# First batch of a retention scan: the state's decay moved to VectorE, half of the key scaling moved to ScalarE

## The chip, the cores and the metric

The kernel runs on one core of a Trainium2 chip. Five engines work side by side, each with its own queue that it takes in order: TensorE (PE in the profile) multiplies matrices into PSUM, VectorE (DVE), ScalarE (ACT) and GpSimd (POOL) work on tiles of 128 partitions, and SyncE (SP) issues the DMAs. They wait for each other by semaphores. The metric is the device time of one launch in microseconds (us), the median of 3 runs.

## The reference

Three blocks follow one another. The first is a causal linear attention with decay over 2 batches, 8 heads, 768 positions and head size 64. The two others are a Fourier mixing block with an MLP and a normalised MLP on the 512 features that result.

```
for b in range(nb):                      # blocks along the sequence
    intra = (qb @ kb.T) * Dmask          # within the block, decay by distance
    intra = intra @ vb
    inter = (qb * lam_pow) @ kv_state    # what earlier blocks left
    out[block] = intra + inter
    kb_dec = kb * rev_pow                # keys, scaled by position in the block
    kv_state = lam_block * kv_state + kb_dec.T @ vb
x = u + mlp(norm(u)), u = out + real(fft2(out))
x = x + mlp(norm(x) * g)
```

## The kernel before, in words

The attention handles chunks of 128 positions, six in each batch; the first batch runs first and alone, in about the first 33 us. For each chunk c of it:

- `attn_a` (lines 338 to 357) scales the keys, kd = k * rev0, by one GpSimd multiply over all 8 heads (line 344), and converts v into a high and a low half (vhl) on ScalarE and VectorE (lines 348, 349).
- `attn_scores` and `attn_x` (lines 363 to 383): TensorE forms the scores of even and odd heads in two PSUM banks. VectorE multiplies each bank with the decay mask (line 377), ScalarE rounds the result to 16 bits (the cast of line 380), GpSimd subtracts to get the low half (line 382). The low half of chunk c and head parity e is `m{c}_{e}` below.
- `attn_s_steps` (from line 470) advances the state, one 64x64 matrix for each head, kept as 128x256 (four pairs of heads). TensorE forms kd.T @ v in PSUM (line 486). In the first batch ScalarE decays the old state beforehand by four 128x64 multiplies, one for each pair (line 477), and VectorE adds the two (line 496). ScalarE then copies the state onto the block diagonals of `diag` (line 501).
- `attn_i_steps` multiplies the next chunk's queries with `diag` (line 399), VectorE scales that into `int` (line 403).
- `attn_o_steps` multiplies m with vhl (line 450), and VectorE writes the sum of that and `int` to u (lines 454, 456).

In the second batch GpSimd does both the key scaling and the decay (line 479); it is not touched.

Up to the output of chunk 3 a scheduler in the framework sets the order on each engine when the program is built; for what is left of the first batch the table ORDER sets it by hand (its token `s` is one step of `attn_s_steps` for chunk 4, O4, O5 and I are steps of the outputs and of the last product), until the first MLP block starts. Behind the change, the order of the instructions on every engine is the same before and after from about the end of the first batch on, and so is the order of all DMAs on SyncE.

Of the kernel before, what the change touches and what calls it, by code (L numbers as in the profile page):

```python
# [14 lines left out]
AF = mybir.ActivationFunctionType  # L15
ALU = mybir.AluOpType
# [3 lines left out]
P = 128  # L20
B, H, S, D = 2, 8, 768, 64
# [105 lines left out]
def tile_retention_fourier_mlp(ctx: ExitStack, tc: tile.TileContext, a: dict, out: bass.AP):  # L127
    nc = tc.nc
    pe, act, dve, pool, sp = nc.tensor, nc.scalar, nc.vector, nc.gpsimd, nc.sync
# [18 lines left out]
    def bank(which, name):  # L148
        return banks[which].tile([P, 512], F32, tag=which, name=name)

    def f32t(name, spare=None):
        if spare is not None:
            return wpool.tile([P, 512], F32, tag=f"w2_{spare}", name=name)
        return fp.tile([P, 512], F32, tag="f", name=name)

    def hl(name):
        return fp.tile([P, 2, 512], F16, tag="f", name=name)
# [17 lines left out]
    loaded = {}  # L175

    def load(b, c, names=("kt", "qt", "v", "k")):
        for nm in names:
            n = ("kt", "qt", "v", "k").index(nm)
            if b == 0 and c >= 2:  # L180
                t = wpool.tile([P, 512], F32, tag=f"w2_{(4 * (c - 1) + n) % 16}", name=f"{nm}{b}_{c}")
            else:
                t = ldp.tile([P, 512], F32, tag="ld", name=f"{nm}{b}_{c}")
            sp.dma_start(t, a[nm][b, c])
            loaded[nm, b, c] = t
# [14 lines left out]
    lc = const.tile([P, H // 2], F32, name="lc")  # L200
# [5 lines left out]
    rev = const.tile([P, H], F32, name="rev")  # L206
    dve.tensor_scalar(rev, last, QS, None, op0=ALU.mult)
    rev0 = const.tile([P, H], F32, name="rev0")
# [129 lines left out]
    def attn_a(b, c, bk):  # L338
        if b > 0 and c + 2 < NCH:
            load(b, c + 2)  # L340
        kd = None
        if c < NCH - 1:
            kd = f32t(f"kd{b}_{c}")
            pool.tensor_tensor(kd.rearrange("p (h d) -> p h d", h=H), loaded["k", b, c].rearrange("p (h d) -> p h d", h=H),  # L344
                               (rev if b else rev0).unsqueeze(2).to_broadcast([P, H, D]), op=ALU.mult)
        v_ = loaded["v", b, c]
        t = hl(f"vhl{b}_{c}")
        act.activation(t[:, 0], v_, AF.Copy, scale=QS)
        dve.scalar_tensor_tensor(t[:, 1], v_, QS, t[:, 0], op0=ALU.mult, op1=ALU.subtract)
        vs[b, c] = t  # L350
        if kd is not None and b == 0:
            ks[b, c] = kd
        elif kd is not None:
            t = hl(f"khl{b}_{c}")
            act.copy(t[:, 0], kd)
            pool.tensor_tensor(t[:, 1], kd, t[:, 0], op=ALU.subtract)
            ks[b, c] = t
# [111 lines left out]

    def attn_s_steps(b, c, bk):  # L470
        new, old = states[c % 2], states[(c - 1) % 2]
        if c > 0:
            dec = stp.tile([P, H // 2 * D], F32, tag="dec", name=f"dec{b}_{c}")
            do, di = (z.rearrange("p (i d) -> p i d", d=D) for z in (dec, old))
            if b == 0:
                for i in range(H // 2):
                    act.activation(do[:, i], di[:, i], AF.Copy, scale=lc[:, i:i + 1])
            else:
                pool.tensor_tensor(do, di, lc.unsqueeze(2).to_broadcast([P, H // 2, D]), op=ALU.mult)
        yield  # L480
        k_ = ks[b, c]
        ps = bank(bk["st"], f"ps_st{b}_{c}")
        for h in range(H):
            (i, e), hc = divmod(h, 2), slice(h * D, (h + 1) * D)
            if b == 0:
                pe.matmul(ps[e * D:(e + 1) * D, i * D:(i + 1) * D], k_[:, hc], loaded["v", b, c][:, hc], start=True, stop=True)
                continue
            for n, (x, y) in enumerate(PASS):
                pe.matmul(ps[e * D:(e + 1) * D, i * D:(i + 1) * D], k_[:, x, hc], vs[b, c][:, y, hc],
                          start=n == 0, stop=n == 2)  # L490
        yield
        psv = ps[:, :H // 2 * D]
        if c == 0:
            dve.tensor_copy(new, psv)
        else:
            dve.tensor_tensor(new, psv, dec, op=ALU.add)
        yield
        if b == 0:
            for e in range(2):
                r = slice(e * D, (e + 1) * D)  # L500
                act.copy(diag[c % 2][r, :, e * D:(e + 1) * D], new[r].rearrange("p (i d) -> p i d", d=D))
        yield

    def attn_c(b, c, bk):
        run(attn_o_steps(b, c, bk))
        if c < NCH - 1:
            run(attn_s_steps(b, c, bk))
# [729 lines left out]
    def attn_seq(b, bk):  # L1237
        seq = {"ab": [(attn_a, 0), (attn_a, 1), (attn_b, 0)], "ba": [(attn_b, 0), (attn_a, 0), (attn_a, 1)],
               "aba": [(attn_a, 0), (attn_b, 0), (attn_a, 1)]}[AO]
        for c in range(NCH):  # L1240
            seq.append((attn_c, c))
            if c + 2 < NCH:
                seq.append((attn_a, c + 2))
            if c + 1 < NCH:
                seq.append((attn_b, c + 1))
                seq.append((attn_i, c + 1))
        return [lambda f=f, c=c: f(b, c, bk) for f, c in seq]
# [41 lines left out]
    def eng(n):  # L1289
        return pool if n in ONPOOL.split() else dve  # L1290

    wide = {}
    chains = {"s": lambda: attn_s_steps(0, 4, bk0), "O4": lambda: attn_o_steps(0, 4, bk0),
              "O5": lambda: attn_o_steps(0, 5, bk0), "I": lambda: attn_i_steps(0, 5, bk0), "R": lambda: row_fold(0)}
    for x in range(2):
# [85 lines left out]
    n = t + DC + DFO  # L1381
# [107 lines left out]
```

## Time and profile before

| | |
|---|---|
| median of 3 runs | 583.66 us (583.55 to 583.71) |
| profiled execution, its own time | 584.53 us |
| its span, first to last instruction | 582.7 us |
| TensorE busy | 564.7 us, 97% |
| VectorE busy | 405.3 us, 70% |
| GpSimd busy | 341.6 us, 59% |
| ScalarE busy | 303.0 us, 52% |

The table is over the whole span. The first 33 us look otherwise: in them GpSimd is nearly as busy as TensorE, and VectorE follows closely, so a share of the whole span says little about the stage that is changed. The profiled execution took 584.53 us, 1.83 us more than its span and 0.87 us more than the median; sums from its rows are made against its own time.

### The profile page before, as it was taken

What the parts mean: (1) busy time and instruction counts of PE and PEld (TensorE: products, weight loads), DVE (VectorE), ACT (ScalarE), POOL (GpSimd) and SP (SyncE); (2) the same over time, 40 slices, a digit from 0 to 9 for tenths busy, and PEclk for the clock granted to TensorE, in tenths of its full rate; (3) what the DMA queues carried; (4) which work ended last, traced back from release to release, by engine and by line L of the source; (5) the groups of instructions that cost most, each with busy time, mean ns of one, the idle gap of its engine ahead of it and who ended that gap; (6) DMA issues with size and microseconds to landing.
All of it is one profiled execution on the core that took longest, in us unless ns stands there. A gap on an engine that the chain in (4) does not pass through costs nothing.

```text
span 582.7 us, 12211 instructions
## 1 busy us (share of the span) xinstructions
PE 564.7 (97%) x4718; PEld 385.0 (66%) x4718; DVE 405.3 (70%) x921; ACT 303.0 (52%) x624; POOL 341.6 (59%) x364
## 2 busy tenths in 40 slices
PE   7989998999999999999999999999999999999997
PEld 4745654666554555677777667666777788878884
DVE  6898898867876449678677766656756665756544
ACT  4867779743232333465597888954242453223320
POOL 7825699985553565365366877754196676223511
PEclk9998999999999999999999999999999999999999
DMA  8999079960000011243365453400120025002001
GB/s 281 369 362 368 19 253 253 334 206 23 1 0 1 10 38 27 74 127 109 83 183 171 131 183 125 141 20 1 55 56 1 19 91 56 2 1 78 34 1 55
DMA packets 47018, 63.26 MB, mean 109 GB/s; under 512 B 26225, under 2 KB 29167, under 8 KB 46959
## 3 DMA queue, kind: packets, MB, share of 16 engines
q1 hardware_dynamic: 46142, 62.27, 34.4%
q8 instruction: 37, 0.61, 0.4%
q10 hardware_dynamic: 816, 0.21, 0.2%
q14 instruction: 23, 0.18, 0.1%
HBM read 52.23 MB, written 6.29 MB: 100 GB/s over the span
## 4 chain that ended last, share of the span: by engine, by line
PE 63%; DVE 12%; POOL 12%; ACT 6%; issue 5%; DMA 1%; SPq 0%; DVEq 0%; POOLq 0%; ACTq 0%
PE ps_y L919 25%; PE ps L868 21%; PE ps_h L759 5%; POOL w L332 4%; POOL m L382 3%; PE ps_y L966 2%; DVE wr L792 1%; PE ps_d L558 1%; PE ps_b L966 1%; PE ps_a L966 1%; POOL kd L344 1%; PE ps_h L749 1%; ACT half L304 1%; DVE tr L815 1%; ACT w L330 1%
## 5 line engine op out<-in xcount | busy, mean ns | idle before, releaser
L919 PE MATMUL ps_y<-w,h 128*128 128x512 f16 (+1 forms) x1026 | 248.1, 377 | 1.7 <-ACT h L904 1.1
L919 PEld LDWEIGHTS <-h 128*128 128x128 f16 x1032 | 98.2, 98 | 88.8 <-ACT h L904 2.5
L868 PEld LDWEIGHTS <-sw 128*128 128x128 f16 x1104 | 94.6, 98 | 20.5 <-issue 2.6
L868 PE MATMUL ps<-th,sw 128*128 128x192 f16 x756 | 86.0, 246 | 1.6 <-DVE wf L307 0.7
L332 POOL TENSOR_TENSOR w<-wf,w 128x512 f16<-128x512 f32 x58 | 66.8, 1159 | 26.8 <-ACT w L330 26.6
L868 PEld LDWEIGHTS <-w 128*128 128x128 f16 x828 | 71.0, 98 | 11.2 <-issue 0.2
L759 PE MATMUL ps_h<-unT,w 128*128 128x384 f16 x396 | 72.3, 326 | 0.7 <-ACT w L330 0.7
L868 PE MATMUL ps<-unT,w 128*128 128x192 f16 x552 | 61.9, 246 | 0.0
L759 PEld LDWEIGHTS <-w 128*128 128x128 f16 x396 | 37.6, 98 | 29.4 <-ACT w L330 1.6
L804 POOL TENSOR_TENSOR sw<-ws,sw 128x512 f16<-128x512 f32 x32 | 37.0, 1174 | 21.2 <-ACT sw L803 21.2
L330 ACT CAST w<-wf 128x512 f16<-128x512 f32 x58 | 35.3, 611 | 12.3 <-DVE wf L317 9.3
L1154 ACT ACTIVATE h<-ps 128x384 f16<-128x384 f32 x44 | 21.7, 496 | 34.3 <-DVE ps L1161 29.7
L382 POOL TENSOR_TENSOR m<-m,m 128x512 f16<-128x512 f32 x24 | 31.7, 1336 | 7.1 <-ACT m L380 5.1
L307 DVE SCALAR_TENSOR_TENSOR wf<-ws,ps_w 128x512 int32<-128x512 int32 x34 | 23.2, 685 | 17.2 <-ACT ps_w L305 6.9
L701 POOL TENSOR_TENSOR rs<-rs,neghalf 128x1 f32<-128x1 f32 x24 | 14.3, 601 | 35.2 <-DVE rs L699 35.2
L833 POOL TENSOR_TENSOR th<-ts,th 128x384 f16<-128x384 f32 x22 | 20.5, 951 | 24.0 <-ACT th L832 22.8
L905 DVE SCALAR_TENSOR_TENSOR h<-ps,h 128x384 f16<-128x384 f32 x48 | 25.6, 553 | 12.7 <-ACT h L904 12.2
L1183 POOL TENSOR_TENSOR hh<-s,hh 128x256 f16<-128x256 f32 x22 | 14.3, 675 | 32.9 <-ACT hh L1182 30.9
L722 POOL TENSOR_TENSOR uns<-un,uns 128x512 f16<-128x512 f32 x21 | 25.2, 1199 | 12.9 <-ACT uns L721 12.9
L904 ACT ACTIVATE h<-ps 128x384 f16<-128x384 f32 x48 | 22.4, 486 | 19.6 <-DVE ps L898 16.0
L774 DVE SCALAR_TENSOR_TENSOR h<-ps_h,h 128x384 f16<-128x384 f32 x36 | 19.7, 549 | 18.1 <-ACT h L773 18.0
L868 PE MATMUL ps<-unT,sw 128*128 128x192 f16 x276 | 30.3, 246 | 0.0
(223 smaller groups left out, 1040.3 us busy)
## 6 DMA issues: line engine op xcount, KB each, us to landing
ws<-in_w SPq DMA_DIRECT2D x25, 511.8 KB, 5.0
ws<-in_w2b SPq DMA_DIRECT2D x16, 511.8 KB, 4.0
ws<-in_w1b SPq DMA_DIRECT2D x16, 511.8 KB, 3.9
kt<-in_kt SPq DMA_DIRECT2D x12, 256.0 KB, 6.3
qt<-in_qt SPq DMA_DIRECT2D x12, 256.0 KB, 5.5
v<-in_v SPq DMA_DIRECT2D x12, 256.0 KB, 5.3
k<-in_k SPq DMA_DIRECT2D x12, 256.0 KB, 4.8
pre<-in_w SPq DMA_DIRECT2D x4, 511.8 KB, 9.7
```

What stands on the lines that cost most here:

```text
L307: dve.scalar_tensor_tensor(ti, raw[:, :, 0], 13, part.bitcast(I32), op0=ALU.logical_shift_right, op1=ALU.bitwise_or)
L330: act.copy(hi, t)
L332: gate["lo"] = pool.tensor_tensor(lo, t, hi, op=ALU.subtract)
L382: pool.tensor_tensor(t[:, 1], m32, t[:, 0], op=ALU.subtract)
L722: pool.tensor_tensor(s_[:, 1], un, s_[:, 0], op=ALU.subtract)
L759: pe.matmul(ps, w[:, i, k, fo:fo + P], x[:, j, k, :], start=n == 0, stop=n == 11)
L804: pool.tensor_tensor(lo, z, hi, op=ALU.subtract)
L868: pe.matmul(ps, lhs, rhs, start=start and n == 0, stop=n == 5, skip_group_check=True)
L904: gate["relu"] = act.activation(hi, z, AF.Relu)
L905: dve.scalar_tensor_tensor(lo, z, 0.0, hi, op0=ALU.max, op1=ALU.subtract)
L919: pe.matmul(ps, h[:, x, j * P:(j + 1) * P], w[:, y, c], start=f == first and n == 0, stop=f == NF - 1 and n == 2, skip_group_check=True)
L966: pe.matmul(ps[:, c], lhs[:, x], rhs[:, y], start=start == 1 and n == 0 and p == 0, stop=n == 2, skip_group_check=True)
```

## The change

For the first batch the separate decay tile is gone: VectorE computes old * lc + PSUM for one pair of heads at a time, four instructions of 128x64 (lc holds one decay factor for each partition and pair). The scaled keys are computed in two parts: heads 4 to 7 by GpSimd in one multiply of 128x256, heads 0 to 3 by ScalarE in four multiplies of 128x64.

```
@@ attn_a
         kd = None
         if c < NCH - 1:
             kd = f32t(f"kd{b}_{c}")
-            pool.tensor_tensor(kd.rearrange("p (h d) -> p h d", h=H), loaded["k", b, c].rearrange("p (h d) -> p h d", h=H),
-                               (rev if b else rev0).unsqueeze(2).to_broadcast([P, H, D]), op=ALU.mult)
+            ko, ki = (z.rearrange("p (h d) -> p h d", h=H) for z in (kd, loaded["k", b, c]))
+            r_, n = (rev, 0) if b else (rev0, H // 2)
+            pool.tensor_tensor(ko[:, n:], ki[:, n:], r_[:, n:].unsqueeze(2).to_broadcast([P, H - n, D]), op=ALU.mult)
+            for h in range(n):
+                act.activation(ko[:, h], ki[:, h], AF.Copy, scale=r_[:, h:h + 1])
@@ attn_s_steps
         new, old = states[c % 2], states[(c - 1) % 2]
-        if c > 0:
+        if c > 0 and b > 0:
             dec = stp.tile([P, H // 2 * D], F32, tag="dec", name=f"dec{b}_{c}")
             do, di = (z.rearrange("p (i d) -> p i d", d=D) for z in (dec, old))
-            if b == 0:
-                for i in range(H // 2):
-                    act.activation(do[:, i], di[:, i], AF.Copy, scale=lc[:, i:i + 1])
-            else:
-                pool.tensor_tensor(do, di, lc.unsqueeze(2).to_broadcast([P, H // 2, D]), op=ALU.mult)
+            pool.tensor_tensor(do, di, lc.unsqueeze(2).to_broadcast([P, H // 2, D]), op=ALU.mult)
...
         if c == 0:
             dve.tensor_copy(new, psv)
+        elif b == 0:
+            for i in range(H // 2):
+                r = slice(i * D, (i + 1) * D)
+                dve.scalar_tensor_tensor(new[:, r], old[:, r], lc[:, i:i + 1], psv[:, r], op0=ALU.mult, op1=ALU.add)
         else:
             dve.tensor_tensor(new, psv, dec, op=ALU.add)
```

The scheduler places the new instructions and moves some of the old ones. Three places matter. The first is the start of ScalarE's queue. In the names the first number is the chunk (vhl_0 belongs to chunk 0, m_0_1 to chunk 0 and odd heads), the last one is the buffer. A wait on DMAHW5 is one for v of chunk 0, a wait on DMAHW6 one for k of chunk 0. Before:

```order
L348 ACT_TABLE_LOAD
L348 ACTIVATE vhl_0_205<-v_0_125 128x512 [waits DMAHW5_49]
L380 CAST m_0_0_225<-m_0_0_0_221 128x512 [waits DVE_49]
L380 CAST m_0_1_228<-m_0_0_1_223 128x512 [waits DVE_49]
L348 ACTIVATE vhl_1_233<-v_1_142 128x512 [waits DMAHW1_49]
L501 COPY diag<-state_161 64x4x64 [waits DVE_49]
```

The same place now:

```order
L348 ACT_TABLE_LOAD [waits DMAHW6_49]
L348 ACTIVATE kd_0_203<-k_0_127,rev_154 128x64 [waits DVE_49]
L348 ACTIVATE kd_0_203<-k_0_127,rev_154 128x64 x3
L351 ACTIVATE vhl_0_209<-v_0_125 128x512 [waits DMAHW5_49]
L383 CAST m_0_0_229<-m_0_0_0_225 128x512 [waits DVE_49]
L383 CAST m_0_1_232<-m_0_0_1_227 128x512 [waits DVE_49]
L348 ACTIVATE kd_1_235<-k_1_144,rev_154 128x64 [waits DMAHW2_49]
```

The four multiplies on k of chunk 0 stand in front of v and of the first cast, and the load of ScalarE's function table, which waited for nothing, now stands behind the wait for k. The second place is GpSimd, from the first scaled keys to the low halves of chunk 2. Before:

```order
L344 TENSOR_TENSOR kd_0_203<-k_0_127,rev_154 128x512 [waits DMAHW6_49]
L382 TENSOR_TENSOR m_0_0_225<-m_0_0_0_221,m_0_0_225 128x512 [waits Activation_49]
L344 TENSOR_TENSOR kd_1_231<-k_1_144,rev_154 128x512 [waits DMAHW2_49]
L382 TENSOR_TENSOR m_0_1_228<-m_0_0_1_223,m_0_1_228 128x512 [waits Activation_49]
L344 TENSOR_TENSOR kd_2_274<-k_2_174,rev_154 128x512 [waits DMAHW6_49]
L382 TENSOR_TENSOR m_1_0_296<-m_0_1_0_292,m_1_0_296 128x512 [waits Activation_49]
L344 TENSOR_TENSOR kd_3_396<-k_3_182,rev_154 128x512 [waits DMAHW2_49,PE_49,Pool_49]
L382 TENSOR_TENSOR m_1_1_299<-m_0_1_1_294,m_1_1_299 128x512 [waits Activation_49]
L382 TENSOR_TENSOR m_2_0_418<-m_0_2_0_414,m_2_0_418 128x512 [waits Activation_49,Pool_49]
L382 TENSOR_TENSOR m_2_1_421<-m_0_2_1_416,m_2_1_421 128x512 [waits Activation_49]
L344 TENSOR_TENSOR kd_4_474<-k_4_315,rev_154 128x512 [waits DMAHW6_49,Pool_49]
```

The same place now:

```order
L346 TENSOR_TENSOR kd_0_203<-k_0_127,rev_154 128x256 [waits DMAHW6_49]
L385 TENSOR_TENSOR m_0_0_229<-m_0_0_0_225,m_0_0_229 128x512 [waits Activation_49]
L385 TENSOR_TENSOR m_0_1_232<-m_0_0_1_227,m_0_1_232 128x512 [waits Activation_49]
L346 TENSOR_TENSOR kd_1_235<-k_1_144,rev_154 128x256 [waits DMAHW2_49]
L346 TENSOR_TENSOR kd_2_282<-k_2_174,rev_154 128x256 [waits DMAHW6_49]
L385 TENSOR_TENSOR m_1_0_308<-m_0_1_0_304,m_1_0_308 128x512 [waits Activation_49]
L346 TENSOR_TENSOR kd_3_406<-k_3_182,rev_154 128x256 [waits DMAHW2_49,Pool_49]
L385 TENSOR_TENSOR m_1_1_311<-m_0_1_1_306,m_1_1_311 128x512 [waits Activation_49]
L346 TENSOR_TENSOR kd_4_486<-k_4_327,rev_154 128x256 [waits DMAHW6_49,Pool_49]
L385 TENSOR_TENSOR m_2_0_432<-m_0_2_0_428,m_2_0_432 128x512 [waits Activation_49]
```

The keys of chunk 1 moved behind both low halves of chunk 0, the keys of chunk 4 ahead of those of chunk 2. The third place is VectorE around the first state that is decayed. Before:

```order
L494 COPY state_161<-ps_st_0_262 128x256 [waits PE_49]
L349 SCALAR_TENSOR_TENSOR vhl_1_233<-v_1_142,vhl_1_233 128x512 [waits DMAHW1_49,Activation_49]
L496 TENSOR_TENSOR state_162<-ps_st_1_384,dec_1_379 128x256 [waits PE_49,Activation_49]
L377 SCALAR_TENSOR_TENSOR m_0_1_0_292<-ps_s_1_0_279,mask 128x512
L377 SCALAR_TENSOR_TENSOR m_0_1_1_294<-ps_s_1_1_280,mask 128x512
```

The same place now:

```order
L493 COPY state_161<-ps_st_0_270 128x256 [waits PE_49]
L352 SCALAR_TENSOR_TENSOR vhl_1_241<-v_1_142,vhl_1_241 128x512 [waits DMAHW1_49,Activation_49]
L457 TENSOR_SCALAR u_119<-ps_o_0_244 128x512 [waits PE_49]
L497 SCALAR_TENSOR_TENSOR state_162<-state_161,lc,ps_st_1_391 128x64 [waits DVE_49,PE_49,Pool_49]
L497 SCALAR_TENSOR_TENSOR state_162<-state_161,lc,ps_st_1_391 128x64 x3
L380 SCALAR_TENSOR_TENSOR m_0_1_0_304<-ps_s_1_0_291,mask 128x512
```

The output of chunk 0 (u) moved ahead of the state of chunk 1, and the state is four instructions instead of one.

## Rows read from the trace of the kernel before

**Rows 1.** Busy time by stretches: stretch, length, each engine's busy us, TensorE's granted clock, DMA share, GB/s.

```profile
33.00:45.00 12.00, 10.29 (x53) 4.89 (x49) 11.55 (x30) 7.03 (x13) 2.16 (x5) 1.00 1.01 391
60.00:100.00 40.00, 38.27 (x261) 21.84 (x261) 35.51 (x64) 32.92 (x63) 34.97 (x38) 1.00 0.61 168
54.50:57.90 3.40, 3.27 (x21) 2.83 (x22) 2.50 (x8) 2.30 (x5) 0.56 (x1) 0.50 1.01 390
```

**Rows 2.** Timeline of VectorE: start, us, line, operation, count [idle before <-releaser].

```profile
21.06 1.29 DVE L377 SCALAR_TENSOR_TENSOR m<-ps_s,mask 128x512 f32<-128x512 f32 x2 [0.21 <-POOL m L382]
...
24.76 0.69 DVE L403 TENSOR_TENSOR int<-ps_i,lp 128x512 f32<-128x512 f32 x1 [0.35 <-POOL m L382]
...
28.79 1.29 DVE L377 SCALAR_TENSOR_TENSOR m<-ps_s,mask 128x512 f32<-128x512 f32 x2 [0.34 <-PE ps_s L370]
29.99 0.41 DVE L496 TENSOR_TENSOR state<-ps_st,dec 128x256 f32<-128x256 f32 x1
...
33.49 0.69 DVE L456 SCALAR_TENSOR_TENSOR u<-ps_o,int 128x512 f32<-128x512 f32 x1
```

**Rows 3.** Chain of waits that ended last: start, us, what.

```profile
18.31 1.11 POOL m L382
19.42 0.46 issue
19.87 2.27 POOL m L382 x2
```

**Rows 4.** Timeline of GpSimd.

```profile
16.18 1.16 POOL L382 TENSOR_TENSOR m<-m,m 128x512 f16<-128x512 f32 x1 [1.99 <-PE ps_st L486]
17.31 1.04 POOL L344 TENSOR_TENSOR kd<-k,rev 128x512 f32<-128x512 f32 x1
...
23.11 2.72 POOL L382 TENSOR_TENSOR m<-m,m 128x512 f16<-128x512 f32 x2
```

**Rows 5.** Timeline of ScalarE.

```profile
1.65 1.28 ACT L348 ACT_TABLE_LOAD   x1 [1.65 <-PEq L1474]
...
7.24 0.63 ACT L348 ACTIVATE vhl<-v 128x512 f16<-128x512 f32 x1 [4.30 <-DMA v<-in_v]
8.64 0.62 ACT L380 CAST m<-m 128x512 f16<-128x512 f32 x1 [0.78 <-DVE m L377]
...
12.13 1.06 ACT L477 ACTIVATE dec<-state,lc 128x64 f32<-128x64 f32 x4
13.10 0.62 ACT L348 ACTIVATE vhl<-v 128x512 f16<-128x512 f32 x1
13.69 0.82 ACT L501 COPY diag<-state 64x256 f32<-64x256 f32 x2
...
15.50 1.12 ACT L380 CAST m<-m 128x512 f16<-128x512 f32 x2
...
30.63 0.81 ACT L501 COPY diag<-state 64x256 f32<-64x256 f32 x2
```

**Rows 6.** Line 479, the second batch's decay: duration in ns min/median/max, first and last start.

```profile
L479 POOL TENSOR_TENSOR dec<-state,lc x4: 602/608/612, 116.2 to 146.7; 128x256 f32<-128x256 f32 x4
```

**Rows 7.** Timeline of VectorE, two small operations of the same kind in a later stage.

```profile
467.24 0.28 DVE L1174 SCALAR_TENSOR_TENSOR s<-ps,s 128x128 f32<-128x128 f32 x1
467.44 0.28 DVE L1175 SCALAR_TENSOR_TENSOR s<-ps,s 128x128 f32<-128x128 f32 x1
```

**Rows 8.** The loads of k up to 12 us: issue and time to landing.

```profile
L184 SPq DMA_DIRECT2D k<-in_k x4: 327/371/432, 2.7 to 10.5; - x4
...
DMA to landing us min/median/max: 4.4/4.8/5.1
```

**Rows 9.** Timeline of TensorE.

```profile
25.89 0.73 PE L450 MATMUL ps_o<-vhl,m 128*128 128x64 f16 x19 [0.57 <-POOL m L382]
...
54.63 1.11 PE L734 MATMUL ps_l<-expo,un 128*128 128x128 f32 x4 [0.62 <-ACT un L713]
...
58.69 0.61 PE L734 MATMUL ps_l<-expo,un 128*128 128x128 f32 x4
```

## The prediction

> **What bounds the kernel now.** I read the busy table by stretches first. Behind 60 us TensorE works 38.27 of 40 us, and from 33 to 45 us VectorE works 11.55 of 12 [rows 1]: whoever delays the end of the first stage delays the end. The change touches only the first stage, which ends when VectorE writes the last rows of u at 33.49 us [rows 2]. So I asked, in the chain of waits, what holds that stage: for most of 16 to 26 us it is GpSimd, which computes the low halves of the masked scores (m) and, between them, the scaled keys (kd) [rows 3, 4]. That argues for taking work off GpSimd. Then I read the timelines of ScalarE and VectorE, because the work has to go somewhere: ScalarE runs without a gap from 12.13 us until past the first casts at 15.50 us [rows 5], and GpSimd's largest idle time, 1.99 us before 16.18 us [rows 4], ends 0.68 us after such a cast starts. GpSimd is therefore fed by ScalarE at the very place where the new work is put.
>
> **The change part by part.**
>
> Keys on GpSimd: five multiplies of 128x512 at 1.04 us [rows 4] become 128x256. This form with its repeated scale stands in the second batch at 0.61 us [rows 6]; I take it, bounds 0.52 (half) and 1.04. Gross gain 5 x 0.43 = 2.15 us of GpSimd.
>
> Keys on ScalarE: five groups of four 128x64 multiplies. The removed decays have exactly this form, 1.06 us for four, and the next instruction starts 0.97 us after the first [rows 5]. Five groups come, four decay groups go: +0.97 us of ScalarE in all. What matters is where. Ahead of the first cast nothing of this stood before; now a whole group does.
>
> State on VectorE: one 128x256 add of 0.41 us [rows 2] becomes four 128x64 operations, which this trace does not show. The nearest rows are 128x128 ones of the same kind, 0.28 us long and 0.20 us apart [rows 7]. With the 64 columns fewer, some 0.07 us each at about 1 ns a column, that makes 3 x 0.13 + 0.21 = 0.60 us; bounds 0.42 (as now) and 3 x 0.20 + 0.28 = 0.88. The Trainium skill (VectorE: DVE Perf Modes, sections Side-by-side: where the cycles go, and Rules for kernel authors) speaks against splitting: about 150 cycles of set-up for every operation, so count operations. By it the four would take an estimated 0.9 us; the trace disagrees for this chip, since its 128x128 operations start every 0.20 us, and by the skill the sum below would be 0.6 us larger.
>
> The start, step by step. The first ScalarE instruction used to wait for v; now it is the group on k of chunk 0. k is issued at 2.7 us and lands at most 5.1 us later [rows 8]: 7.8 us. The order shows that wait ahead of the table load. Before, the load ran at 1.65 us, 1.28 us long, while ScalarE had nothing to do [rows 5]; now it starts when k has landed. So: 7.85 + 1.28 + 0.97 (four multiplies) + 0.59 (v, 13.10 to 13.69) = 10.7 us for the first cast, where it was 8.64 [rows 5]. It is 2.0 us late, of which 1.28 is the load. Bounds: with the load out of the way 0.75; nothing in the rows lets it come earlier than before.
>
> From there to the cast of chunk 1. GpSimd starts 0.68 us behind a cast [rows 4, 5]: 11.35. Two low halves at 1.25 each (pairs take 2.27 to 2.72 [rows 3, 4]): 13.85. TensorE ends the 19 matmuls that need them in 0.73 [rows 9], with handoffs 14.8. On VectorE the copy of u for chunk 0 (0.60) now stands ahead of the state of chunk 1, so the state waits for those matmuls too; with its 0.60 it is there at 16.0. ScalarE copies it to diag (0.82 [rows 5]) and reaches the cast at 16.9, GpSimd at 17.55, where it was 16.18. GpSimd's idle time has swallowed 0.65 of the 2.0, and 1.4 us remain. ScalarE's own queue alone would arrive there at about 16.3 or a little before, so it is not what ends last.
>
> From there to the end of the stage. GpSimd: low half 1.25, key 0.61, low half 1.25, key 0.61, low half 1.25 = 4.97, to 22.5 us. Before, the same low half of chunk 2 ended when VectorE started at 21.06 [rows 2]; one key of 1.04 and a gap of 0.46 lay in between [rows 3, 4]. The key of chunk 4 has moved ahead of it, so nothing is won here: 1.5 us late. VectorE starts its mask for chunk 3 on that low half, and needs 3.70 us to the scaled product of chunk 3 at 24.76 [rows 2]; one score matmul of 0.14 has moved ahead on TensorE: 1.65 late. Then VectorE's queue runs through to the state of chunk 4. Its idle 0.34 us ahead of 28.79 [rows 2] closes, the state costs 0.19 more: 1.5 late. Diag of chunk 4 began 0.23 us after the state ended, since casts stood before it [rows 2, 5]; now it follows at once: 1.3 us late, and so is all behind it. The decay of chunk 4 and the key of chunk 4, both removed or halved, lay beside other work and return nothing.
>
> Sum. The profiled execution took 584.53 us with a span of 582.7; its own time becomes 585.8. The median of the runs is 0.87 below it: 583.66 + 1.3 = **585.0 us**, 0.2% slower. With the low ends (small operations 0.42, low halves 1.14, keys 0.52) the delay is about 0.6, with the high ends (0.88, 1.36, 0.8) about 2.2.
>
> **Rivals.**
>
> A. GpSimd is the bound throughout and the late start disappears in its 1.99 us idle time [rows 4]. Then the four keys behind the first low half give 4 x 0.43 = 1.7 us: 582.0 us, faster. For it: the chain of waits names GpSimd [rows 3]. Against it: the idle time ends on a cast, and this cast is later by more than the copies in front of it can give back. It decides whether GpSimd starts its first low half of chunk 1 by about 16.2 us.
>
> B. The table load is not held by the wait, or runs early as before. Then the first cast is 0.75 late, less than the 1.99 us of idle time, the chain above loses 1.28 at its head, and the end is where it was: 583.7 us. For it: the load itself needs no data. Against it: ScalarE takes its instructions in order, and the wait stands in front.
>
> C. The load costs more than its 1.28 us when work queues directly behind it. The rows can't show this: ScalarE sat idle from 2.93 us until v came [rows 5]. One more load's length gives 586.3 us. The Trainium skill (ScalarE: Activation LUTs, section What ACT_TABLE_LOAD costs) states 1283 ns, as in the trace, and a drain of about 1.38 us for every switch; by that drain the time would be an estimated 586.4 us, and no row here shows it.
>
> D. TensorE is idle longer at 8 to 14 us, and its clock falls. It fell once in this run: 54.5 to 57.9 us at 0.50, the lower of its two levels (1.2 GHz), with TensorE busy 3.27 of 3.40 there [rows 1], and four matmuls took 1.11 us instead of 0.61 [rows 9]. In the first stage that could double some 2.5 us of work, of which I count half as hidden: 1.2 us more, 586.2 us.
>
> **How the numbers follow.** My forecast 0.58 (584.3 to 585.9), A 0.08, B 0.12, C 0.08, D 0.14. A measurement of this kernel can tell about 0.2%, 1.17 us, from no change; that line lies at 584.83, close under the forecast. Of the forecast's 0.58 I put 0.37 above the line and 0.21 within; C and D lie above, B within, A below but for 0.01. Slower 0.59, same 0.34, faster 0.07. The range leaves out A and about half of C and D: 583.5 to 586.4 us.
>
> **What would show it.** Right: the table load starting near 7.9 us and the first cast at 10.5 to 11 us; GpSimd's first low half of chunk 1 near 17.5 us with its idle time before it still there; keys of 0.6 us on GpSimd; four state operations within 0.5 to 0.9 us; the last u of the stage near 34.8 us, and after it the same distances as now. Wrong: a table load at 1.65 us (B), a gap of over a microsecond behind it (C), a granted clock under 1.00 before 33 us (D), or GpSimd working from 16.2 us without a gap (A). A late stage that is made up again before 100 us would break the first step, that the stage sets the end.

## The result and the profile after

| | before | now |
|---|---|---|
| median of 6 runs each | 583.68 us (583.55 to 583.78) | 587.78 us (585.89 to 588.54) |
| profiled execution, own time | 584.53 us | 585.89 us |
| its span | 582.7 us | 584.1 us |
| its mean granted TensorE clock | 0.997 | 1.000 |

The change makes the kernel slower by 0.6%: ratio 1.0061, 95% interval 1.0049 to 1.0072. The time lies 2.8 us above the forecast and 1.4 us above the range. Two things in the table need an answer. The profiled execution is the fastest of the six, so its trace cannot show all of the loss. And the six runs spread over 2.65 us where those of before spread over 0.23. Their mean granted clocks go with it: 1.000 at 585.89, 0.997 at 586.38, 0.988 to 0.994 at 587.46 to 588.54.

First what that fastest profile shows of the stage. ScalarE's timeline (start, us, line, operation, count, and in brackets the idle time before it and what ended it):

```profile
7.97 1.28 ACT L348 ACT_TABLE_LOAD   x1 [7.97 <-DMA k<-in_k]
9.27 1.06 ACT L348 ACTIVATE kd<-k,rev 128x64 f32<-128x64 f32 x4
...
10.76 1.12 ACT L383 CAST m<-m 128x512 f16<-128x512 f32 x2
...
16.24 0.82 ACT L504 COPY diag<-state 64x256 f32<-64x256 f32 x2 [0.54 <-DVE state L497]
17.08 1.14 ACT L383 CAST m<-m 128x512 f16<-128x512 f32 x2
...
32.73 0.82 ACT L504 COPY diag<-state 64x256 f32<-64x256 f32 x2
```

The load waits for k, the multiplies follow it at once, and the first cast starts at 10.76 instead of 8.64 us [rows 5]. GpSimd's timeline:

```profile
11.44 2.27 POOL L385 TENSOR_TENSOR m<-m,m 128x512 f16<-128x512 f32 x2 [2.85 <-ACT m L383]
...
17.78 1.24 POOL L385 TENSOR_TENSOR m<-m,m 128x512 f16<-128x512 f32 x1 [2.48 <-ACT m L383]
18.98 0.61 POOL L346 TENSOR_TENSOR kd<-k,rev 128x256 f32<-128x256 f32 x1
```

The low half of chunk 1 starts 1.60 us later than at 16.18 [rows 4], and the idle time ahead of it is now put down to the cast at 17.08. VectorE's timeline, with the rows that answer to [rows 2]:

```profile
14.53 0.69 DVE L457 TENSOR_SCALAR u<-ps_o 128x512 f32<-128x512 f32 x1 [0.27 <-PE ps_o L453]
15.35 0.85 DVE L497 SCALAR_TENSOR_TENSOR state<-state,lc,ps_st 128x64 f32<-128x64 f32 x4
...
22.88 0.69 DVE L380 SCALAR_TENSOR_TENSOR m<-ps_s,mask 128x512 f32<-128x512 f32 x1 [0.26 <-POOL m L385]
...
27.06 0.69 DVE L406 TENSOR_TENSOR int<-ps_i,lp 128x512 f32<-128x512 f32 x1 [0.74 <-POOL m L385]
...
31.85 0.84 DVE L497 SCALAR_TENSOR_TENSOR state<-state,lc,ps_st 128x64 f32<-128x64 f32 x4
...
35.60 0.69 DVE L459 SCALAR_TENSOR_TENSOR u<-ps_o,int 128x512 f32<-128x512 f32 x1
```

The last u comes at 35.60 instead of 33.49 us: the stage is 2.11 us late. The span grew by 1.4 only, since before's profile has a stretch at 0.50 from 54.5 to 57.9 us [rows 1] and this one has none. That stretch is also why before's profiled run stood 0.87 above its median. Against undisturbed runs the two numbers meet: 585.89 - 583.66 = 2.23. Behind the stage nothing is made up: from the start of the last u to the end of the span it is 548.5 us (584.1 - 35.6), and it was 549.2 (582.7 - 33.5) with the stretch at 0.50. The busy time by stretches, columns as in [rows 1], stays near to that of before:

```profile
33.00:45.00 12.00, 9.92 (x63) 5.87 (x64) 11.37 (x27) 7.20 (x14) 3.06 (x6) 1.00 1.03 407
60.00:100.00 40.00, 37.79 (x265) 21.67 (x263) 35.15 (x63) 32.27 (x62) 35.25 (x38) 1.00 0.56 151
```

So the trace explains 2.1 to 2.2 us, and some 2 us more of the median must be looked for in a run that is not the fastest.

### The profile page after: what moved, and what is told of

It reads as the page before. It is cut to its first block, busy times and chain, and to the rows that moved or that the text cites. A ratio compares the mean times of both kernels' runs of the same rounds, so it can differ in the third digit from the quotient of the medians.

```text
span 584.1 us, 12232 instructions
## 1 busy us (share of the span) xinstructions
PE 564.5 (97%) x4718; PEld 384.5 (66%) x4718; DVE 406.5 (70%) x933; ACT 303.7 (52%) x628; POOL 339.2 (58%) x364
## 4 chain that ended last, share of the span: by engine, by line
PE 60%; DVE 13%; POOL 12%; issue 6%; ACT 6%; DMA 2%; SPq 0%; DVEq 0%; POOLq 0%; ACTq 0%
PE ps_y L922 25%; PE ps L871 21%; PE ps_h L762 5%; POOL w L332 4%; POOL m L385 3%; PE ps_y L969 2%; DVE wr L795 1%; PE ps_d L561 1%; PE ps_b L969 1%; PE ps_a L969 1%; POOL kd L346 1%; DVE tr L818 1%; DMA k<-in_k 1%; POOL sw L807 1%; ACT w L330 1%
## 5 line engine op out<-in xcount | busy, mean ns | idle before, releaser
L762 PE MATMUL ps_h<-unT,w 128*128 128x384 f16 x396 | 72.3, 326 | 0.8 <-ACT w L330 0.8
L762 PEld LDWEIGHTS <-w 128*128 128x128 f16 x396 | 37.7, 98 | 29.5 <-ACT w L330 1.7
L1157 ACT ACTIVATE h<-ps 128x384 f16<-128x384 f32 x44 | 21.7, 496 | 34.6 <-DVE ps L1164 30.0
L385 POOL TENSOR_TENSOR m<-m,m 128x512 f16<-128x512 f32 x24 | 30.3, 1280 | 11.6 <-ACT m L383 11.6
```

The lines of the kernel that those rows point to most:

```text
L385: pool.tensor_tensor(t[:, 1], m32, t[:, 0], op=ALU.subtract)
L762: pe.matmul(ps, w[:, i, k, fo:fo + P], x[:, j, k, :], start=n == 0, stop=n == 11)
```

## The experiments

Two theories went in. Start theory: the late start of ScalarE's queue delays the stage, and that is all. Clock theory: the change also lets TensorE's clock fall in most runs (the prediction's rival D), which the first profile happened to miss.

**The changed kernel again (e1_again).** No edit.

> The changed kernel once more, for a second profile of it. Start theory (the stage ends 2.1 us later, 0.7 us of it given back by a missing clock fall in the profiled run): 585.5 to 586 in every run, spread 0.3 us as in the kernel before, granted clock 0.997 or 1.00 in all. Clock theory (the later start lets TensorE's clock fall in most runs, at a place that the first profile missed): median 587 to 588.5, spread over 1 us, mean granted clock 0.988 to 0.997, and the profile shows one or more stretches at 0.50 beside the 54.5 to 57.9 us of the kernel before.

Measured: 588.31 us (587.53 to 589.05), ratio 1.0075 (1.0062 to 1.0088), mean clocks 0.987 to 0.994, as the clock theory said. The profile, of a run of 589.05 us, has three stretches at 0.50 (busy time by stretches: PE, PEld, DVE, ACT, POOL, then the granted clock):

```profile
8.00:11.30 3.30, 1.71 (x24) 1.50 (x26) 1.67 (x3) 3.29 (x8) 0.67 (x2) 1.00 1.06 401
11.32:18.14 6.82, 6.82 (x62) 5.75 (x58) 3.65 (x10) 4.93 (x15) 3.86 (x4) 0.50 1.06 405
35.21:38.62 3.41, 3.41 (x36) 3.10 (x36) 2.06 (x4) 0.19 (x1) 2.06 (x5) 0.50 1.02 412
59.10:62.50 3.40, 3.40 (x23) 2.97 (x24) 2.47 (x8) 2.08 (x4) 0.56 (x1) 0.50 0.49 141
```

0.50 is the lower of the two levels, 1.2 GHz. Beside it the same work of TensorE, here and in the undisturbed profile. The disturbed one:

```profile
9.59 1.28 PE L485 MATMUL ps_st<-v,kd 128*64 128x64 f32 x16 [1.71 <-ACT kd L348]
10.79 1.64 PE L373 MATMUL ps_s<-qt,kt 64*128 64x128 f32 x16
...
14.61 1.20 PE L453 MATMUL ps_o<-vhl,m 128*128 128x64 f16 x19
...
16.36 1.99 PE L402 MATMUL ps_i<-diag,qt 128*128 128x128 f32 x8
...
59.01 1.07 PE L737 MATMUL ps_l<-expo,un 128*128 128x128 f32 x4 [0.62 <-ACT un L716]
...
69.92 2.11 PE L762 MATMUL ps_h<-unT,w 128*128 128x384 f16 x12
```

The undisturbed one:

```profile
9.67 1.28 PE L485 MATMUL ps_st<-v,kd 128*64 128x64 f32 x16 [1.73 <-ACT kd L348]
10.88 1.16 PE L373 MATMUL ps_s<-qt,kt 64*128 64x128 f32 x16
...
13.77 0.73 PE L453 MATMUL ps_o<-vhl,m 128*128 128x64 f16 x19
...
15.16 1.16 PE L402 MATMUL ps_i<-diag,qt 128*128 128x128 f32 x8
...
56.74 0.66 PE L737 MATMUL ps_l<-expo,un 128*128 128x128 f32 x4 [0.62 <-ACT un L716]
...
66.77 2.11 PE L762 MATMUL ps_h<-unT,w 128*128 128x384 f16 x12
```

TensorE stands idle for 1.7 us before the state matmuls, waiting for ScalarE's half of the keys (1.21 us before, for GpSimd's). Some 1.7 us after it resumes, the clock falls and stays down for 6.8 us. The undisturbed run had the same idle time (1.73 us) and no fall, so the idle time goes with the fall in some runs and not in all. What each fall costs is read from VectorE and from the last two rows of each fence:

```profile
33.07 0.84 DVE L497 SCALAR_TENSOR_TENSOR state<-state,lc,ps_st 128x64 f32<-128x64 f32 x4
...
37.88 0.69 DVE L459 SCALAR_TENSOR_TENSOR u<-ps_o,int 128x512 f32<-128x512 f32 x1 [0.59 <-PE ps_o L453]
```

The state of chunk 4 is 1.22 us later than at 31.85: the first fall. The last u is 2.28 later than at 35.60: the second adds 1.06. The row of L737 is 2.27 later, the row of L762 3.15: the third adds 0.88. The spans differ by 587.3 - 584.1 = 3.2. A fall of 6.8 us lowers a run's mean clock by 6.8 x 0.5 / 587 = 0.006; 8 of the 10 runs of this kernel are at 0.994 or lower, of the kernel before 6 of the 61 that were run beside the experiments. (Two falls of 3.4 us give the same mean, which does not say where they were.)

**The table load early (e2_early_load).** A ScalarE instruction that needs no data goes first:

```
+    tick = const.tile([P, 1], F32, name="tick")
+    pool.memset(tick, 0.0)
+    act.activation(tick, tick, AF.Copy)
```

> The changed kernel with a ScalarE activation on a tile of one column ahead of everything, so that the table load runs at about 2 us instead of behind the wait for k; all else in the same order. Start theory: first cast at 9.4 us instead of 10.76, last u of the stage 1.0 to 1.3 earlier, 584.3 to 584.8. Rival (the load is hidden by what GpSimd waits for anyway): last u within 0.3 of 35.6, time as the changed kernel. Clock theory: if the later first casts are what lets the clock fall, the spread shrinks to 0.3 us and the mean granted clock returns to 0.997; if it is something else, median 586 or more and clocks under 0.995 stay.

Measured: 584.95 us (584.58 to 586.28), ratio 1.0023 (1.0014 to 1.0032); six of nine runs at clock 1.000, three at 0.997. ScalarE, then TensorE and VectorE of its profile:

```profile
1.17 1.28 ACT L168 ACT_TABLE_LOAD   x1 [1.17 <-PEq L1480]
...
9.70 1.12 ACT L386 CAST m<-m 128x512 f16<-128x512 f32 x2
```

```profile
8.62 1.28 PE L488 MATMUL ps_st<-v,kd 128*64 128x64 f32 x16 [0.55 <-ACT kd L351]
```

```profile
34.54 0.69 DVE L462 SCALAR_TENSOR_TENSOR u<-ps_o,int 128x512 f32<-128x512 f32 x1
```

The cast and the last u both come 1.06 us earlier: what the early load gives the first cast passes whole to the end of the stage. TensorE's idle time shrinks from 1.73 to 0.55 us, and no run has a mean clock under 0.997. Falls are not gone altogether: this profile has one from 55.7 to 59.1 us, behind the stage, the spread is 1.7 us and not 0.3, and the median lies 0.15 us above the start theory's range. This kernel is still 1.05 us later at the last u than before; the rest of the change costs that much.

**The state part alone (e3_state_alone).** The keys go back to GpSimd for all chunks.

> Only the state part of the change: VectorE decays and adds, the keys all on GpSimd as before; the head of ScalarE's queue is the old one. Start theory: table load at 1.65 us, first cast 8.6, GpSimd's low half of chunk 1 at 16.2 or earlier, last u of the stage 0 to 0.5 late (the four state operations cost 0.44 more each than the add, but 1.06 of decays leave ScalarE): 583.2 to 584.2. Rival (the state part is what costs, 0.85 for 0.41 on VectorE, which is full from 33 us on and close to full before): last u over 1 us late, 584.7 to 586.

Measured: 584.64 us (583.47 to 585.40), ratio 1.0011 (1.0002 to 1.0020). The profile's last u:

```profile
33.17 0.69 DVE L456 SCALAR_TENSOR_TENSOR u<-ps_o,int 128x512 f32<-128x512 f32 x1
```

The stage ends 0.32 us earlier than before. The rival (over 1 us late) falls; the start theory had 0 to 0.5 late, so the state part is better than even that said, and only the time, 584.64, lies above its range. The one run at clock 1.000 took 583.47, but the ten others are at 0.994 to 0.997, and so the median is higher than the stage would make it. The profiled run has the fall at 54.3 to 57.7 us, as before's profile has. That shifting a stage by a few tenths changes how often that fall comes is seen, not explained.

**The key part alone (e4_keys_alone).** The decays and the add stay as before, the keys are split as in the change.

> Only the key part: half of the keys on ScalarE, the decays stay on ScalarE too. Start theory: table load at 8 us, first cast at 10.8, ScalarE 1.06 us fuller for each chunk: last u of the stage 2 to 3.5 us late, 585.5 to 587.5. Rival (state part is what costs): 583.5 to 584.2. Clock theory: the spread of the changed kernel is here too, clocks of 0.988 to 0.997.

Measured: 587.88 us (586.17 to 590.76), ratio 1.0069 (1.0049 to 1.0090). Two runs at clock 1.000 took 586.17 and 586.31, the four others, at 0.988 to 0.994, 587.7 to 590.8. The profile has one fall up to 100 us:

```profile
11.36:18.18 6.82, 6.82 (x62) 5.68 (x58) 3.52 (x7) 6.12 (x19) 4.13 (x5) 0.50 1.06 405
18.20:100.00 81.80, 73.98 (x642) 47.77 (x642) 71.91 (x139) 62.38 (x135) 56.23 (x61) 1.00 0.72 247
```

The key part alone brings both the lateness (the runs at clock 1.000 are 2.4 to 2.5 us above the kernel before) and the fall at the same place; TensorE's idle time ahead of it is 1.72 us. The median lies above the range, as its falls were not counted in it. The profiled run took 588.74, some 2.5 us above those at clock 1.000: here the one fall costs twice the 1.22 us of the first fall above.

**TensorE's idle time filled (e5_filled_gap).** In the changed kernel, behind the first scores, matmuls whose result nobody reads:

```
+            if b == c == 0:
+                fill = bank(bk["st"], "fill")
+                for i in range(24):
+                    pe.matmul(fill[:, :64], warm[:, :P], warm[:, :64], start=True, stop=True)
```

> The changed kernel, its order kept, with 24 small matmuls of 64 columns that feed nothing behind the first scores, where TensorE stands idle for 1.7 us (7.9 to 9.6 us); they fill some 0.9 us of it. Clock theory (that idle time lets TensorE's clock fall at about 11 us): granted clock 1.00 from 8 to 20 us, every run near 585.9, mean clocks of 0.997 to 1.00, all else as late as in the changed kernel. Rival (the fall is let in by the later stage as a whole, or by something else): median 587.5 to 588.5 and the fall from 11.3 to 18.2 us stay.

Measured: 585.92 us (585.75 to 587.18), ratio 1.0039 (1.0026 to 1.0052); clocks 1.000 in three runs, 0.997 in two. TensorE, the stretch in which the clock had fallen, and VectorE of its profile:

```profile
7.75 0.87 PE L377 MATMUL fill<-warm 128*128 128x64 f16 x24
9.54 1.28 PE L489 MATMUL ps_st<-v,kd 128*64 128x64 f32 x16 [0.91 <-ACT kd L348]
```

```profile
11.30:18.10 6.80, 6.29 (x96) 5.01 (x92) 4.91 (x13) 6.17 (x18) 4.31 (x5) 1.00 1.05 404
```

```profile
35.47 0.69 DVE L463 SCALAR_TENSOR_TENSOR u<-ps_o,int 128x512 f32<-128x512 f32 x1
```

This is the deciding run. The stage ends as late as in the changed kernel (35.47 against 35.60), and 0.87 us of matmuls that compute nothing bring the median from 4.1 and 4.5 us above the kernel before to 2.05. The interval lies wholly under that of the changed kernel run again (1.0062 to 1.0088) and touches that of its first six runs (1.0049 to 1.0072). The profile, of a run at clock 1.000, proves little by itself, since the first profile of the changed kernel had no fall either; the weight lies on the runs: none of five at 0.994 or lower, against 8 of 10. The chip does not explain it: of the kernel before, 2 of 17 runs are that low on this run's chip and 1 of 21 on that of the changed kernel run again. So what lies between the forecast mechanism and the median is the clock, and the idle time on TensorE at this place is what lets it fall so often. The two runs at 0.997 took 586.77 and 587.18; where their clock fell is not shown.

**The keys of chunk 0 back on GpSimd (e6_first_keys_back).**

```
-            r_, n = (rev, 0) if b else (rev0, H // 2)
+            r_, n = (rev, 0) if b else (rev0, H // 2 if c else 0)
```

> The changed kernel with the keys of chunk 0 all on GpSimd again; the other four chunks are split as in the change. Head theory (all the loss is at the head of ScalarE's queue): first cast 8.6 us, last u of the stage at 33.5 or earlier, no clock fall before 20 us, 583.0 to 583.8. Rival (the load is only half of the lateness, the rest is the four multiplies for each chunk on ScalarE and the order that they bring): first cast 8.6, last u near 34.5, 584.6 to 585.2.

Measured: 585.90 us (585.37 to 586.19), ratio 1.0031 (1.0019 to 1.0043): neither number. First cast at 8.62 and no fall before 20 us, as both said. But five of six runs are at 0.997, and the profile has a fall from 31.9 to 35.3 us. VectorE and TensorE:

```profile
30.29 0.85 DVE L497 SCALAR_TENSOR_TENSOR state<-state,lc,ps_st 128x64 f32<-128x64 f32 x4
...
35.44 0.69 DVE L459 SCALAR_TENSOR_TENSOR u<-ps_o,int 128x512 f32<-128x512 f32 x1 [0.59 <-PE ps_o L453]
```

```profile
32.04 2.08 PE L402 MATMUL ps_i<-diag,qt 128*128 128x128 f32 x8 [1.15 <-ACT diag L504]
```

Up to the state of chunk 4, where no clock has fallen yet, this gives the split of the lateness: before 29.99, this kernel 30.29, early load 30.80, the change 31.85. So 0.30 us are the other chunks' keys and the state part together, 0.51 the first four multiplies, 1.05 the load. With the state part alone (e3) that state starts at 29.43, 0.56 us earlier than before; if the parts add up, the state part gains 0.56 and the other chunks' keys cost 0.86. The fall then hits eight matmuls on the path (2.08 instead of 1.16 us) and what follows them. It cost this run about 1.4 us: the undisturbed profile has 3.75 us from that state to the last u, this one 5.15.

**The late load alone (e7_late_load_alone).** In the kernel before, one small ScalarE instruction on k and rev0 ahead of v, all else in the old order:

```
+        if b == c == 0:
+            tick = const.tile([P, 1], F32, name="tick")
+            act.activation(tick, loaded["k", 0, 0][:, :1], AF.Copy, scale=rev0[:, :1])
```

> The kernel before, its order kept, with one ScalarE activation of one column on k of chunk 0 in front, so that the table load waits for k as in the change; nothing else is moved and TensorE's first idle time stays 1.2 us. Queue theory (whatever delays the first cast passes through GpSimd to the end of the stage): first cast at 9.9 to 10.1 us, last u of the stage 1.3 late, 585.0. Swallow theory (GpSimd's idle time before 16.18 us takes half, as in the prediction): last u 0.6 late, 584.3. Clock theory: no fall from 11 to 18 us, as TensorE waits for k and GpSimd as before; if it falls nonetheless, 586 to 587.

Measured: 585.91 us (585.86 to 587.40), ratio 1.0042 (1.0029 to 1.0054). ScalarE, GpSimd and VectorE:

```profile
8.06 1.28 ACT L348 ACT_TABLE_LOAD   x1 [8.06 <-DMA k<-in_k]
...
10.08 0.60 ACT L383 CAST m<-m 128x512 f16<-128x512 f32 x1
11.53 0.62 ACT L383 CAST m<-m 128x512 f16<-128x512 f32 x1 [0.85 <-DVE m L380]
...
16.79 1.12 ACT L383 CAST m<-m 128x512 f16<-128x512 f32 x2
```

```profile
17.47 1.16 POOL L385 TENSOR_TENSOR m<-m,m 128x512 f16<-128x512 f32 x1 [2.00 <-PE ps_st L489]
```

```profile
34.77 0.69 DVE L459 SCALAR_TENSOR_TENSOR u<-ps_o,int 128x512 f32<-128x512 f32 x1
```

The second cast of the kernel before:

```profile
10.25 0.62 ACT L380 CAST m<-m 128x512 f16<-128x512 f32 x1 [0.99 <-DVE m L377]
```

The first cast is 1.44 us late and the last u 1.28, as the queue theory said. The low half of chunk 1 is 1.29 us late (16.18 before), and GpSimd's idle time of 2 us ahead of it stands there as before (2.00, 1.99): it looks like slack and gives nothing back. It ends when ScalarE's cast of chunk 1 (16.79, 1.29 late) and TensorE's state matmuls, which the profile names, are done, and both come as late as the start. The 0.15 that is lost on the way is lost before: ScalarE's second cast is only 1.28 late, since the idle time ahead of it shrinks from 0.99 to 0.85. (In the changed kernel the cast of chunk 1 is 1.58 late where the first one was 2.12, and ScalarE's idle time between them is 0.54 in place of 0.99.) The time, 585.91, is 0.9 above the queue theory's 585.0, and no run of the five is at clock 1.000. The profiled run took 1.38 us more than before's, both with one fall between 54 and 60 us. TensorE's first idle time is 1.25 us here, and its clock does not fall at 11 us in the profile; where it fell in the two runs at 0.994 and 0.991 is not shown.

**Two heads, chunks 1 and 4 only (e8_two_heads_twice, e10_two_again).** The state part stays on VectorE:

```
-            r_, n = (rev, 0) if b else (rev0, H // 2)
+            r_, n = (rev, 0) if b else (rev0, 2 if c in (1, 4) else 0)
```

> The state part, and keys of two heads only on ScalarE, for chunks 1 and 4 alone (128x384 on GpSimd there, 128x512 elsewhere). Queue theory: nothing ahead of the first cast, GpSimd 0.2 us less ahead of chunk 1 and of chunk 3's low halves, last u of the stage 1.0 us earlier than in the kernel before (0.7 earlier than with the state part alone): 582.6 to 583.2. Rival (GpSimd's keys lie beside other work): 583.6 to 584.6, as the state part alone.

> The kernel with two heads on ScalarE for chunks 1 and 4 once more, for a narrower interval: 583.0 to 583.5, 0.6 to 0.7 us under the kernel before in runs with the same mean clock, ratio 0.998 to 0.999.

Measured: 583.14 us (583.04 to 583.51) against 583.87, ratio 0.9983 (0.9974 to 0.9992); the second time 583.36 (583.21 to 586.06) against 583.97, ratio 0.9993 (0.9982 to 1.0005). In runs with a mean clock of 0.999 or 1.000 (583.04 to 583.18, then 583.21 to 583.38) it is 0.6 us or a little more under those of the kernel before (583.68 to 583.81 and 583.78 to 583.97, but for one run each). The last u of the first profile:

```profile
32.84 0.69 DVE L459 SCALAR_TENSOR_TENSOR u<-ps_o,int 128x512 f32<-128x512 f32 x1
```

0.65 us earlier than before, where the expectation had 1.0. The gain is small but it is the mechanism that the change meant: work off ScalarE behind the first cast, a little less on GpSimd (a key of 128x384 takes 0.82 us there, one of 128x512 1.04). The second interval includes no change: three of its runs are at 0.994, and its profile, of one of them, has two falls (31.2 to 34.6 and 55.0 to 58.5 us).

**One head (e9_one_head_twice).** The same with one head for the two chunks.

> As the run with two heads on ScalarE for chunks 1 and 4, but with one head (128x448 on GpSimd there). Queue theory, by which ScalarE's queue feeds GpSimd and so less on it is better: last u 0 to 0.25 us earlier than the 32.84 of that run, 582.8 to 583.2. GpSimd theory (the keys taken off it are what pays): 0.1 to 0.3 later, 583.2 to 583.5.

Measured: 583.56 us (583.35 to 585.12), ratio 0.9990 (0.9980 to 1.0000). Its last u:

```profile
33.00 0.69 DVE L459 SCALAR_TENSOR_TENSOR u<-ps_o,int 128x512 f32<-128x512 f32 x1
```

It is 0.16 later than with two heads, and its runs at 0.999 to 1.000 are 0.1 to 0.2 slower than those of two heads on the same chip. That speaks for the GpSimd theory: at this place what is taken off GpSimd pays more than what ScalarE is spared.

## Why the prediction was wrong

**The direction and the first mechanism were right.** The load behind k starts at 7.97 (7.9 said), the first cast at 10.76 (10.7), the low half of chunk 1 at 17.78 (17.55), with its idle time still there, and nothing behind the stage gives it back. The path there is the forecast one too: the copy of u for chunk 0 at 14.53, the state behind it at 15.35, diag at 16.24 after a wait for that state, the cast at 17.08 (16.9 said). In the kernel before, though, GpSimd was not fed by ScalarE alone at this place: [rows 4] name TensorE's state matmuls as what ended its idle time, and they ended within 0.05 us of the cast. Rival A falls: GpSimd does not start by 16.2 us. Rival B falls on the load's start, rival C on the next instruction: it starts at 9.27, 0.02 us after the load's end. The drain that the Trainium skill (ScalarE: Activation LUTs, section What ACT_TABLE_LOAD costs) states for every switch to a different set would by an estimate have moved it to some 10.6; no drain is seen here, nor in the kernel with the early load.

**The step that failed is the one that left TensorE's clock as it was.** The forecast held 0.58 on that, and rival D, the clock falling in the first stage, 0.14. D happened in most runs: 8 of the 10 have a mean clock of 0.994 or lower, the second profile has 0.50 from 11.3 to 18.1 us, and 1.9 us of the median go with it (587.78 - 585.89). Its price for the first fall came out as said, 1.2 us against 1.22, but by luck: D doubled 2.5 us of work and took half, and the fall held 6.82 us of work at half clock, so an estimated 3.4 us were added, of which about a third came through; in the key part alone one such fall cost some 2.5 us. It also came on top of a lateness that was itself too small, and with further falls at 35 and 59 us (1.06 and 0.88 in that profile) that D did not count. Filling the idle time took the runs at 0.994 and lower away and left the lateness, so the two are separate.

**The lateness was under-sized: 1.3 said, 2.1 measured.** The missing 0.8 builds up as 0.23 at the low half of chunk 1, 0.32 at the mask of chunk 3, 0.65 at its scaled product, 0.80 at diag of chunk 4. Two terms make most of it:

- The four state operations: 0.60 taken, 0.85 measured, twice on the path. I had let 64 columns save 0.07 each against the 128-column rows [rows 7]. They save next to nothing:

```profile
L497 DVE SCALAR_TENSOR_TENSOR state<-state,lc,ps_st x16: 266/271/279, 15.3 to 32.4; 128x64 f32<-128x64 f32 x16
```

  0.27 us each and four in 0.85, hence 0.19 apart, where 128 columns took 0.28 and 0.20. The Trainium skill (VectorE: DVE Perf Modes, section Rules for kernel authors) had said to count operations, and the estimate of 0.9 worked out from it, which I set aside, was the better one; the upper bound of 0.88 held.
- From the mask of chunk 3 to its scaled product I moved the 3.70 us of before along and added 0.15; now it is 4.18 (22.88 to 27.06). The order of VectorE's work between the two had changed, and 0.74 us of it is a wait for GpSimd that was 0.35.

**The sum with both mended.** 583.66 + 2.1 = 585.8, which the runs at clock 1.000 show (585.89, and 585.75 to 585.92 with the idle time filled), and about 2 for the falls: 587.8. That 2 is what is left over and not a sum of its own: the one profile with all three falls adds 3.15 us, and how many of them the median run had is not shown.

**What stays open.** In the changed kernel the same idle time of 1.7 us is followed by a fall in one profile and by none in the other; what decides it is not shown. Nor is why some orders bring a fall at 32 or at 54 us. An early load together with a filled idle time was not tried.

## What to carry to other kernels

An instruction that now stands first in a queue takes all that the queue used to do in idle time along behind its wait: look for the table load, and give ScalarE something that needs no data at the start (here 3.4 us of the median: 588.31 to 584.95). A wait of TensorE on a small part of another engine's work can be paid twice, as here: once as lateness, once in the clock. So compare its idle times before and after, not its busy share alone. And when runs of one kernel spread ten times as far as those of the other, take a second profile before explaining the first: the fastest run shows only the part that is always there.

## What was not expected of the hardware

- TensorE's clock fell behind an idle time of 1.71 us, while 1.15 to 1.25 us at the same place in other kernels (1.21 before, 1.25 in the late load alone) left it at 1.00 there in their profiles. It does not always fall: 1.73 us in the first profile of the changed kernel did not bring it down. The fall came while TensorE worked, 1.7 us after it had resumed, and lasted 6.8 us at 0.50.
- 24 matmuls of 64 columns that compute nothing, 0.87 us in all, save some 2 us of the median.
- On VectorE, in this form, halving 128 columns to 64 changed the distance of starts from 0.20 to 0.19 us only.
- The table load takes 1.28 us and the next instruction starts 0.01 to 0.02 us behind it.
